# One exponential per attention chunk in a fused attention and gated FFN kernel: differences and sums on VectorE, weight words converted in place

## The chip, the cores and the metric

The kernel runs on one core of a Trainium2 chip. The metric is device time in microseconds (us) of one launch. The kernel before takes 1119.18 us, the median of 3 runs (1118.94 to 1120.06).

The engines go by the profile's names: PE is TensorE (PEld its weight loads), DVE is VectorE, ACT is ScalarE, POOL is GpSimd, SP is SyncE, whose queue issues the DMAs.

## The reference

```python
# q, k, v: (8, 8, 576, 64) float32, S = 576, pool = 8, Sp = 72
k_p = k.reshape(B, H, Sp, pool, D).mean(axis=3)
v_p = v.reshape(B, H, Sp, pool, D).mean(axis=3)
scores = scale * np.matmul(q, k_p.transpose(0, 1, 3, 2))
scores = scores - np.max(scores, axis=-1, keepdims=True)
attn = np.exp(scores)
attn = attn / (np.sum(attn, axis=-1, keepdims=True) + 1e-09)
out = np.matmul(attn, v_p).astype(np.float32)
# x = out with heads side by side: (4608, 512)
a = x @ w_a            # (512, 1536)
b = x @ w_b
return (a * b @ w_out).astype(np.float32)
```

Keys and values are averaged in groups of eight, so each of the 64 pairs of batch and head attends with 576 queries to 72 keys. The 4608 tokens of 512 numbers then go through an FFN with two input matrices, whose products are multiplied, and one output matrix. The three weight matrices arrive as float64 and are used as float32.

## The kernel before, in words

**Precision.** Every matmul runs in the float32r format, with each operand split into a high part (a cast by ScalarE) and a low part (the difference, on VectorE or GpSimd), and three products: high x high, high x low, low x high. That is why things come in pairs: qh and ql, xh and xl, hh and hl, jha and jla.

**The FFN loop.** The tokens are worked through in 9 tiles of 512 (NT), each in 12 steps f of 128 inner columns. In `ffn_in` a step makes psa (12 matmuls of 512 columns, lines 522 to 524) and psb (12 more). ScalarE copies psa to h (L527), VectorE multiplies psb into h (L500, in `gated`), ScalarE casts hh (L503), VectorE makes hl (L170, the line of every low part). `ffn_out` adds the product with the output matrix to four PSUM banks acc (12 matmuls, lines 543 to 545), one step late.

**The attention.** The queries of a batch are cut into five chunks of 128 or 64 rows (`chunks_of`); there are 40 chunks i. Chunks 0 to 3 belong to tile 0 and are done ahead of the FFN loop (`early`), chunks 4 to 8 to tile 1, and chunks 9 to 39 to the tiles from 2 on: 25 of these have 128 rows and six have 64. The generator `chunk(i)` does one chunk: it loads the queries (tile qraw), makes qh (L356) and ql, and then the scores. Two head groups g (two heads each) share one PSUM tile psc: three matmuls of 144 columns for each g (L379), whose loaded operand is the queries and whose moving operand is kdiag, the pooled keys with a high part (w = 0) and a low part (w = 1). VectorE takes the maximum of each head (L388) and scales it by -1/8 (L389); ScalarE then makes one exponential for each head with that bias, which also adds up the head's sum z (L392). After both pairs VectorE adds 1e-9 to z and inverts it (L399, L400), GpSimd (VectorE for two early chunks) multiplies s by it (L402), ScalarE casts the high parts pr and rem (L411, L413), and GpSimd makes their low parts. Three rounds of transposes follow (ptr, L447, copied to p by ScalarE, L448), then the product with the values vdiag and vrem (po, lines 480 to 483), and xh and xl (L491, L170).

The banks for psc, ptr and po come from the tag "att" with two buffers (the early chunks take psc from "acc", with four). A tile is free again when its last reader is done.

**Keys and values.** `load_keys(b)` and `load_values(b)` load a batch's keys and values and pool them on VectorE (L253, L305). At the end `load_values` makes vwide (L314), vdiag (L328) and vrem on VectorE in three neighbouring steps.

**Weights.** `convert_weights` runs in tile 0 for each matrix (a, b, o): a DMA brings 512 KB of 64-bit words into `words`, one for each f; ScalarE shrinks the high words into a temporary `wmag` (L210) and the low words into `wlow` (L211); VectorE masks and shifts `wmag` into the weights' place (L212), adds the sign (L216) and adds the low word (L221). The next words of a matrix are asked for only after L216. `split_weight` makes the high and low parts of a weight; for the matrices a and b in tile 0 the low part (jla, jlb) is VectorE's, else GpSimd's (L235).

**What sets the order.** The program is written out in one fixed order for every engine. The class `Chains` holds all generators as chains: each runs until a `yield`, which gives the number of steps it sleeps, or until `yield PE`, by which it asks for a place among the matmuls. The FFN loop calls `chains.step()` once every six of its matmuls, six times an f, and each call takes up the chains that are due and one that asks for PE. So one more `yield 1` in a chunk moves all that follows it on by one step, behind what other chains and the FFN issue on the same engine.

Of the kernel before, what the change touches and what calls it, by code (L numbers as in the profile page):

```python
# [11 lines left out]
I32 = mybir.dt.int32  # L12
# [40 lines left out]
BLOCK, BLOCK_LATER = 256, 384  # L53

NTMP = 6

AHEAD = 2

# [12 lines left out]
class Chains:  # L71
# [9 lines left out]
    def mark(self, *what):  # L81
        self.done.add(what)
# [30 lines left out]
def attn_moe_kernel(ctx: ExitStack, tc: tile.TileContext, q, k, v, vr, wa, wb, wo, out):  # L113
# [80 lines left out]
    def convert_weights(name, j, first):  # L194

        def load_words(f):
            nc.sync.dma_start(area[name], w_dram[name][:, f, :].bitcast(I32))  # L200

        load_words(0)
        yield first
        for f in range(NF):
            words = area[name].rearrange("p (c w) -> p c w", w=2)
            hi, lo = words[:, :, 1], words[:, :, 0]
            w = raw[name][:, f, :]
            wi = w.bitcast(I32)
            low, mag = tmp(f"wlow_{name}{f}", I32), tmp(f"wmag_{name}{f}")
            nc.scalar.activation(mag, hi.bitcast(F32), AF.Abs, scale=SHRINK)  # L210
            nc.scalar.activation(low, lo.bitcast(U32), AF.Copy, scale=2.0**-29)  # L211
            nc.vector.tensor_scalar(  # L212
                out=wi, in0=mag.bitcast(I32), scalar1=0x0FFFFFFF, scalar2=3, op0=ALU.bitwise_and, op1=ALU.logical_shift_left
            )
            yield 1
            nc.vector.scalar_tensor_tensor(  # L216
                out=wi, in0=hi, scalar=-(1 << 31), in1=wi, op0=ALU.bitwise_and, op1=ALU.bitwise_or
            )
            if f + 1 < NF:
                load_words(f + 1)  # L220
            nc.vector.tensor_tensor(out=wi, in0=wi, in1=low, op=ALU.add)  # L221
            mark("weight", name, f)
            yield 2

            while f + 1 >= AHEAD and (len(begun) <= f + 1 - AHEAD or chains.now < begun[f + 1 - AHEAD] + 2 * j):
                yield 1
# [116 lines left out]
    def chunk(i):  # L343
# [22 lines left out]
        z = sb.tile([P, H], F32, tag="z", name=f"z_{i}")  # L366
        hk = 2 * SP

        for g0 in range(0, NK, 2):
            yield from wait(("keys", b, g0))  # L370
            yield PE
            if first:
                pt = ps.tile([P, 512], F32, tag="acc", name=f"psc_{i}_{g0}", bufs=4)
            else:
                pt = ps.tile([P, 512], F32, tag="att", name=f"psc_{i}_{g0}", bufs=2)
            for j in range(2):
                g = g0 + j
                for x, (qq, w) in enumerate(((qh, 0), (qh, 1), (ql, 0))):
                    nc.tensor.matmul(  # L379
                        pt[:n, j * hk:(j + 1) * hk],  # L380
                        qq[:, g, :n],
                        kd[:, g, w].rearrange("p e s -> p (e s)"),
                        start=(x == 0),
                        stop=(x == 2),
                    )
            hs = slice(2 * g0, 2 * g0 + 4)
            scores = pt[:n, :2 * hk].rearrange("p (h s) -> p h s", h=4)
            nc.vector.tensor_reduce(out=m[:n, hs], in_=scores, axis=AX.X, op=ALU.max)  # L388
            nc.vector.tensor_scalar_mul(m[:n, hs], m[:n, hs], -SCALE)  # L389
            for j in range(4):  # L390
                h = 2 * g0 + j
                nc.scalar.activation(  # L392
                    s[:n, h], scores[:, j], AF.Exp, bias=m[:n, h:h + 1], scale=SCALE, accum_out=z[:n, h:h + 1]
                )
        mark("scores", i)


        yield 1
        nc.vector.tensor_scalar_add(z[:n], z[:n], 1e-9)  # L399
        nc.vector.reciprocal(z[:n], z[:n])  # L400
        yield 1
# [254 lines left out]
```

## Time and profile before

| | |
|---|---|
| median of 3 runs | 1119.18 us (1118.94 to 1120.06) |
| the profiled execution | 1116.74 us, of which the span of its instructions is 1115.0 |
| mean granted clock of TensorE | 0.986 |
| instructions | 14406 |
| share of the chain that ended last | PE 78%, DVE 13%, ACT 6%, issue 2%, DMA 1% |
| DMA | 59.64 MB, mean 53 GB/s |

The profile is one execution. Its span runs from the first instruction to the end of the last. Row counts such as x432 are instructions; "idle before" is the time the engine stood still just ahead of them, with what ended it. The chain is followed back from the last instruction, at each step to what released it. Three stages are told apart: 0 to 60 us (the front: early chunks, first weight words), 60 to 209 us (tile 0) and 209 us to the end. Line numbers here and in the prediction are those of the kernel before.

### The profile page before, as it was taken

To read this page: it belongs to the slowest core of one execution; us is meant where nothing else is said; L and a number is where in the kernel's file an instruction comes from. 1 tells how busy PE (TensorE), PEld (TensorE's weight loads), DVE (VectorE), ACT (ScalarE), POOL (GpSimd) and SP (SyncE) were. 2 spreads that over 40 slices of the span, in tenths; PEclk is the share of its full clock that TensorE was granted. 3 is DMA by queue.
4 is the path that set the end of the run, shared out by engine and by line. 5 is a ranking of instruction groups with operands and counts; after the bars stand their busy time and mean duration, and the time that the engine had idled before them with its cause. 6 is when DMAs were issued, how large, how long until landed. Compare 5 with 4: busy or idle time off the path is not lost.

```text
span 1115.0 us, 14406 instructions
## 1 busy us (share of the span) xinstructions
PE 1045.9 (94%) x5088; PEld 870.9 (78%) x5088; DVE 543.8 (49%) x839; ACT 594.8 (53%) x1651; POOL 538.6 (48%) x441
## 2 busy tenths in 40 slices
PE   4387888999998999999999999999999999999998
PEld 4276666888887888888887888888887888888887
DVE  7688888632455225632456335643356333332111
ACT  5756766545555455554556455554555455453332
POOL 7102322555555555555556455545546555554442
PEclk9989889999999999999999999999999999999999
DMA  6454443210112001300030003200211020001001
GB/s 209 131 160 123 124 150 126 73 42 1 55 42 85 1 1 41 130 1 1 22 115 14 1 2 102 68 1 1 69 55 48 1 66 1 2 1 38 1 1 38
DMA packets 29879, 59.64 MB, mean 53 GB/s; under 512 B 7120, under 2 KB 7120, under 8 KB 29808
## 3 DMA queue, kind: packets, MB, share of 16 engines
q1 hardware_dynamic: 29808, 58.73, 16.5%
q8 instruction: 40, 0.66, 0.3%
q14 instruction: 31, 0.25, 0.1%
HBM read 49.28 MB, written 9.44 MB: 53 GB/s over the span
## 4 chain that ended last, share of the span: by engine, by line
PE 78%; DVE 13%; ACT 6%; issue 2%; DMA 1%; SPq 0%; DVEq 0%; ACTq 0%
PE psb L522 8%; PE psa L522 8%; PE psa L524 8%; PE psa L523 8%; PE acc L543 8%; PE acc L544 8%; PE acc L545 8%; PE psb L524 8%; PE psb L523 7%; PE psc L379 3%; ACT s L392 3%; DVE vdiag L328 2%; PE ptr L447 2%; DVE vrem L170 1%; DVE h L500 1%
## 5 line engine op out<-in xcount | busy, mean ns | idle before, releaser
L500 DVE TENSOR_TENSOR h<-psb,h 128x512 f32<-128x512 f32 x108 | 74.5, 690 | 310.7 <-PE psb L524 310.6
L170 POOL TENSOR_TENSOR jlb<-wb_raw,jhb 128x512 fp32r<-128x512 f32 x96 | 125.1, 1303 | 201.2 <-ACT jhb L233 201.2
L170 POOL TENSOR_TENSOR jlo<-wo_raw,jho 128x512 fp32r<-128x512 f32 x108 | 152.7, 1414 | 81.0 <-ACT jho L233 51.8
L522 PE MATMUL psb<-xh,jhb 128*128 128x512 f32 x432 | 177.8, 412 | 1.3 <-DVE h L500 1.3
L524 PE MATMUL psb<-xh,jlb 128*128 128x512 f32 x432 | 171.5, 397 | 1.8 <-DVE jlb L170 1.8
L522 PE MATMUL psa<-xh,jha 128*128 128x512 f32 x432 | 172.3, 399 | 0.0
L543 PE MATMUL acc<-jho,hh 128*128 128x512 f32 x432 | 171.5, 397 | 0.0
L527 ACT COPY h<-psa 128x512 f32<-128x512 f32 x108 | 63.5, 588 | 201.9 <-PE psa L524 188.4
L523 PE MATMUL psb<-xl,jhb 128*128 128x512 f32 x432 | 170.8, 395 | 0.0
L524 PE MATMUL psa<-xh,jla 128*128 128x512 f32 x432 | 170.1, 394 | 0.0
L523 PE MATMUL psa<-xl,jha 128*128 128x512 f32 x432 | 169.6, 393 | 0.0
L544 PE MATMUL acc<-jlo,hh 128*128 128x512 f32 x432 | 169.5, 392 | 0.0
L545 PE MATMUL acc<-jho,hl 128*128 128x512 f32 x432 | 169.2, 392 | 0.0
L392 ACT ACTIVATE s<-psc,m 128x72 f32<-128x72 f32 (+1 forms) x320 | 97.9, 318 | 133.1 <-DVE m L389 131.7
L170 POOL TENSOR_TENSOR jla<-wa_raw,jha 128x512 fp32r<-128x512 f32 x96 | 138.4, 1442 | 44.1 <-ACT jha L233 43.7
L402 POOL TENSOR_TENSOR s<-s,z 128x576 f32<-128x576 f32 (+1 forms) x38 | 46.1, 1213 | 223.7 <-PE psb L524 141.0
L170 DVE TENSOR_TENSOR hl<-h,hh 128x512 fp32r<-128x512 f32 x108 | 125.8, 1165 | 38.2 <-ACT hh L503 38.0
L503 ACT CAST hh<-h 128x512 fp32r<-128x512 f32 x108 | 67.1, 622 | 89.4 <-DVE h L500 89.2
L524 PEld LDWEIGHTS psb<-xh,jlb 128*128 128x128 f32 x432 | 82.4, 191 | 20.8 <-DVE jlb L170 2.7
L524 PEld LDWEIGHTS psa<-xh,jla 128*128 128x128 f32 x432 | 81.9, 190 | 17.5
L545 PEld LDWEIGHTS acc<-jho,hl 128*128 128x128 f32 x432 | 81.8, 189 | 17.4
L543 PEld LDWEIGHTS acc<-jho,hh 128*128 128x128 f32 x432 | 81.9, 190 | 16.2
(84 smaller groups left out, 1806.3 us busy)
## 6 DMA issues: line engine op xcount, KB each, us to landing
out<-y SPq DMA_DIRECT2D x36, 256.0 KB, 2.1
kraw<-in_k SPq DMA_DIRECT2D x28, 288.0 KB, 3.4
vraw<-in_v SPq DMA_DIRECT2D x28, 256.0 KB, 3.3
qraw<-in_q SPq DMA_DIRECT2D x28, 256.0 KB, 3.7
words<-in_wa SPq DMA_DIRECT2D x12, 512.0 KB, 3.7
words<-in_wb SPq DMA_DIRECT2D x12, 512.0 KB, 3.6
words<-in_wo SPq DMA_DIRECT2D x12, 512.0 KB, 3.6
vraw<-in_vr SPq DMA_DIRECT2D x14, 192.0 KB, 2.7
```

Of the source, the lines that this page charges most:

```text
L170: eng.tensor_tensor(out=lo, in0=src, in1=hi.bitcast(F32), op=ALU.subtract)
L392: nc.scalar.activation(s[:n, h], scores[:, j], AF.Exp, bias=m[:n, h:h + 1], scale=SCALE, accum_out=z[:n, h:h + 1])
L402: (nc.vector if first and i % 2 else nc.gpsimd).tensor_tensor(out=s[:n], in0=s[:n], in1=z[:n].unsqueeze(2).broadcast_to([n, H, SP]), op=AL ...
L500: nc.vector.tensor_tensor(out=h, in0=pt, in1=h, op=ALU.mult)
L503: nc.scalar.copy(hh, h)
L522: nc.tensor.matmul(pt, wh[:, c], xh[:, kk], start=(kk == 0), stop=False)
L523: nc.tensor.matmul(pt, wh[:, c], xl[:, kk], start=False, stop=False)
L524: nc.tensor.matmul(pt, wl[:, c], xh[:, kk], start=False, stop=(kk == NK - 1))
L527: nc.scalar.copy(h, pt)
L543: nc.tensor.matmul(acc[c], hh[:, cs], wh, start=(f == 0), stop=False)
L544: nc.tensor.matmul(acc[c], hh[:, cs], wl, start=False, stop=False)
L545: nc.tensor.matmul(acc[c], hl[:, cs], wh, start=False, stop=(f == NF - 1))
```

## The change

There are three parts.

1. In `convert_weights` ScalarE writes the shrunk high words into the weights' own place, and VectorE masks and shifts them there. The temporary `wmag` is gone.
2. The softmax: the new `less_max` takes the maximum of each head and subtracts it, both on VectorE, and writes the differences to s. Then one exponential over all eight heads (576 numbers a row) is made by ScalarE in place, and VectorE adds up z.
3. Chunks from 9 on (SUMMED) make their scores otherwise: one matmul of 288 columns takes qh with the high and the low keys side by side, one of 144 takes ql with the high keys on top of the first half, and VectorE adds the two halves of the bank into s (a reduction over pairs). Each g has a bank of its own, two g are taken in one place among the matmuls. `less_max` then runs once on s.

The words given with the change also name lo parts of two matrices on VectorE in the first tile; that line (L235) is the same in both kernels.

```diff
+SUMMED = 9
...
-            low, mag = tmp(f"wlow_{name}{f}", I32), tmp(f"wmag_{name}{f}")
-            nc.scalar.activation(mag, hi.bitcast(F32), AF.Abs, scale=SHRINK)
+            low = tmp(f"wlow_{name}{f}", I32)
+            nc.scalar.activation(w, hi.bitcast(F32), AF.Abs, scale=SHRINK)
...
-                out=wi, in0=mag.bitcast(I32), scalar1=0x0FFFFFFF, scalar2=3, op0=ALU.bitwise_and, op1=ALU.logical_shift_left
+                out=wi, in0=wi, scalar1=0x0FFFFFFF, scalar2=3, op0=ALU.bitwise_and, op1=ALU.logical_shift_left
...
-            nc.vector.tensor_reduce(out=m[:n, hs], in_=scores, axis=AX.X, op=ALU.max)
-            nc.vector.tensor_scalar_mul(m[:n, hs], m[:n, hs], -SCALE)
-            for j in range(4):
-                h = 2 * g0 + j
-                nc.scalar.activation(
-                    s[:n, h], scores[:, j], AF.Exp, bias=m[:n, h:h + 1], scale=SCALE, accum_out=z[:n, h:h + 1]
+        def less_max(hs, src):
+            nh = hs.stop - hs.start
+            nc.vector.tensor_reduce(out=m[:n, hs], in_=src, axis=AX.X, op=ALU.max)
+            nc.vector.tensor_tensor(
+                out=s[:n, hs], in0=src, in1=m[:n, hs].unsqueeze(2).broadcast_to([n, nh, SP]), op=ALU.subtract
+            )
+
+        if i < SUMMED:
...
+                less_max(slice(2 * g0, 2 * g0 + 4), pt[:n, :2 * hk].rearrange("p (h s) -> p h s", h=4))
+        else:
+            for g in range(NK):
+                yield from wait(("keys", b, g - g % 2))
+                if g % 2 == 0:
+                    yield PE
+                pt = ps.tile([P, 512], F32, tag="att", name=f"psc_{i}_{g}", bufs=2)
+                nc.tensor.matmul(
+                    pt[:n, :2 * hk], qh[:, g, :n], kd[:, g].rearrange("p w e s -> p (w e s)"), start=True, stop=False
                 )
+                nc.tensor.matmul(
+                    pt[:n, :hk], ql[:, g, :n], kd[:, g, 0].rearrange("p e s -> p (e s)"), start=False, stop=True
+                )
+                nc.vector.tensor_reduce(
+                    out=s[:n, 2 * g:2 * g + 2, :].rearrange("p h s -> p (h s)"),
+                    in_=pt[:n, :2 * hk].rearrange("p (w c) -> p c w", w=2),
+                    axis=AX.X,
+                    op=ALU.add,
+                )
+                if g % 2 and g < NK - 1:
+                    yield 1
+            yield 1
+            less_max(slice(0, H), s[:n])
         mark("scores", i)
...
         yield 1
+        nc.scalar.activation(s[:n], s[:n], AF.Exp, scale=SCALE)
+        yield 1
+        nc.vector.tensor_reduce(out=z[:n], in_=s[:n], axis=AX.X, op=ALU.add)
         nc.vector.tensor_scalar_add(z[:n], z[:n], 1e-9)
         nc.vector.reciprocal(z[:n], z[:n])
```

How the change moves instructions is seen in the order in which each engine gets them. A row is the line, the operation, output and inputs (with running numbers) and the shape of the output. On TensorE, at the first place of scores of a chunk in the third tile, before (psc are the scores of two head groups, psa and psb the FFN's):

```order
L524 MATMUL psa_5_3437<-xh_2027,jla_3385 128x512
L379 MATMUL psc_0_3451<-kdiag_74,qh_3418 128x144 x2
L379 MATMUL psc_0_3451<-kdiag_74,ql_3419 128x144
L379 MATMUL psc_0_3451<-kdiag_74,qh_3418 128x144 x2
L379 MATMUL psc_0_3451<-kdiag_74,ql_3419 128x144
L522 MATMUL psa_5_3437<-xh_2027,jha_3384 128x512
```

The same place after, with the second one, six FFN matmuls on:

```order
L403 MATMUL psc_0_3319<-kdiag_74,qh_3286 128x288
L406 MATMUL psc_0_3319<-kdiag_74,ql_3287 128x144
L403 MATMUL psc_1_3323<-kdiag_74,qh_3286 128x288
L406 MATMUL psc_1_3323<-kdiag_74,ql_3287 128x144
L549 MATMUL psa_5_3305<-xh_1952,jha_3252 128x512
L550 MATMUL psa_5_3305<-xl_1953,jha_3252 128x512
L551 MATMUL psa_5_3305<-xh_1952,jla_3253 128x512
L549 MATMUL psa_5_3305<-xh_1952,jha_3252 128x512
L550 MATMUL psa_5_3305<-xl_1953,jha_3252 128x512
L551 MATMUL psa_5_3305<-xh_1952,jla_3253 128x512
L403 MATMUL psc_2_3337<-kdiag_74,qh_3286 128x288
L406 MATMUL psc_2_3337<-kdiag_74,ql_3287 128x144
```

Six matmuls in one bank have become four in two banks, and psc_2 takes the bank of psc_0 again.

On VectorE, at the end of the values load in the third tile beside a chunk of 64 rows, before (hl and h are the FFN's, z the sums of the chunk, vwide, vdiag and vrem the values load's):

```order
L170 TENSOR_TENSOR hl_3011<-h_2971,hh_3010 128x512
L399 TENSOR_SCALAR z_3021<-z_3021 64x8
L400 RECIPROCAL z_3021<-z_3021 64x8
L314 SCALAR_TENSOR_TENSOR vwide_3085<-vp_2842,mask 96x256 x2
L328 SCALAR_TENSOR_TENSOR vdiag_76<-vp_2842,vdiag_76 64x4x64 x2
L170 TENSOR_TENSOR vrem_2841<-vwide_3085,vrem_2841 32x512
L500 TENSOR_TENSOR h_3107<-psb_1_3109,h_3107 128x512
```

And after (L172 is the line of the low parts, L527 that of h):

```order
L172 TENSOR_TENSOR hl_2873<-h_2844,hh_2872 128x512
L316 SCALAR_TENSOR_TENSOR vwide_2934<-vp_2714,mask 96x256 x2
L330 SCALAR_TENSOR_TENSOR vdiag_76<-vp_2714,vdiag_76 64x4x64 x2
L409 TENSOR_REDUCE s_2881<-psc_2_2960 64x144
L409 TENSOR_REDUCE s_2881<-psc_3_2964 64x144
L373 TENSOR_REDUCE m_2882<-s_2881 64x8
L374 TENSOR_TENSOR s_2881<-s_2881,m_2882 64x576
L172 TENSOR_TENSOR vrem_2713<-vwide_2934,vrem_2713 32x512
L527 TENSOR_TENSOR h_2974<-psb_1_2976,h_2974 128x512
L425 TENSOR_REDUCE z_2883<-s_2881 64x8
L426 TENSOR_SCALAR z_2883<-z_2883 64x8
L427 RECIPROCAL z_2883<-z_2883 64x8
```

The z steps have moved from ahead of the values load to behind the next h, and four operations on the scores stand between vdiag and h.

On ScalarE, where it first comes to weight words, before (p are the transposed weights of attention, pr and rem their high parts):

```order
L448 COPY p_0_283<-ptr_0_335 128x4x128
L448 COPY p_0_311<-ptr_1_343 128x4x128
L448 COPY p_0_325<-ptr_2_349 96x2x128
L411 CAST pr_353<-s_250 128x512
L413 CAST rem_354<-s_250 128x2x32 x2
L210 ACTIVATE wmag_a_359<-words 128x512
```

And after:

```order
L475 COPY p_0_263<-ptr_0_311 128x4x128
L475 COPY p_0_289<-ptr_1_319 128x4x128
L212 ACTIVATE wa_raw<-words 128x512
L213 ACTIVATE wlow_a_325<-words 128x512
L475 COPY p_0_300<-ptr_2_330 96x2x128
L438 CAST pr_334<-s_235 128x512
```

The first words stand ahead of the third copy of transposes and of the last early chunk's casts.

More of the change, by code (lines that the diff above doesn't have):

```diff
@@ L367, in chunk @@
         hk = 2 * SP
[L369 to L389, printed above, removed]
-            for j in range(4):
-                h = 2 * g0 + j
-                nc.scalar.activation(
-                    s[:n, h], scores[:, j], AF.Exp, bias=m[:n, h:h + 1], scale=SCALE, accum_out=z[:n, h:h + 1]
-                )
@@ new lines, in less_max @@
+        def less_max(hs, src):
[5 more added lines that the diff above has]
+        if i < SUMMED:
+            for g0 in range(0, NK, 2):
+                yield from wait(("keys", b, g0))
+                yield PE
+                if first:
+                    pt = ps.tile([P, 512], F32, tag="acc", name=f"psc_{i}_{g0}", bufs=4)
+                else:
+                    pt = ps.tile([P, 512], F32, tag="att", name=f"psc_{i}_{g0}", bufs=2)
+                for j in range(2):
+                    g = g0 + j
+                    for x, (qq, w) in enumerate(((qh, 0), (qh, 1), (ql, 0))):
+                        nc.tensor.matmul(
+                            pt[:n, j * hk:(j + 1) * hk],
+                            qq[:, g, :n],
+                            kd[:, g, w].rearrange("p e s -> p (e s)"),
+                            start=(x == 0),
+                            stop=(x == 2),
+                        )
+                less_max(slice(2 * g0, 2 * g0 + 4), pt[:n, :2 * hk].rearrange("p (h s) -> p h s", h=4))
+        else:
+            for g in range(NK):
+                yield from wait(("keys", b, g - g % 2))
+                if g % 2 == 0:
+                    yield PE
+                pt = ps.tile([P, 512], F32, tag="att", name=f"psc_{i}_{g}", bufs=2)
+                nc.tensor.matmul(
+                    pt[:n, :2 * hk], qh[:, g, :n], kd[:, g].rearrange("p w e s -> p (w e s)"), start=True, stop=False
+                )
+                nc.tensor.matmul(
+                    pt[:n, :hk], ql[:, g, :n], kd[:, g, 0].rearrange("p e s -> p (e s)"), start=False, stop=True
[5 more added lines that the diff above has]
+                    op=ALU.add,
+                )
+                if g % 2 and g < NK - 1:
+                    yield 1
+            yield 1
+            less_max(slice(0, H), s[:n])
```

## The prediction

> **What bounds the kernel now.** I read the page first, then busy time by stage, then the chain and the waits of each stage.
>
> ```profile
> span 1115.0 us, 14406 instructions
> PE 1045.9 (94%) x5088; PEld 870.9 (78%) x5088; DVE 543.8 (49%) x839; ACT 594.8 (53%) x1651; POOL 538.6 (48%) x441
> ```
>
> The first row is the span, the second each engine's busy time. TensorE (PE) is busy 94% of the span, VectorE (DVE) and ScalarE (ACT) about half. But 69 us of TensorE's time are idle, and an average doesn't say where. The stages do (start:end, length, busy time of PE, PEld, DVE, ACT, POOL, then granted clock, DMA share, GB/s):
>
> ```profile
> 0.00:60.00 60.00, 25.43 (x121) 23.30 (x122) 42.11 (x79) 35.82 (x121) 24.03 (x33) 1.00 0.55 178
> 60.00:209.00 149.00, 127.42 (x591) 101.60 (x591) 123.68 (x207) 100.79 (x268) 36.96 (x29) 0.92 0.40 125
> 209.00:1115.00 906.00, 893.04 (x4380) 745.99 (x4378) 378.02 (x554) 458.22 (x1263) 477.64 (x380) 1.00 0.10 34
> ```
>
> Three kernels in one. In the last 906 us TensorE idles 13 us: only fewer matmuls, or the few stalls, can gain there. In the front (60 us, before the first FFN matmul) and in the first tile (149 us) TensorE idles 35 and 22 us; there VectorE is the fullest engine, or nearly so (42 of 60 us, 124 of 149), and what it or ScalarE loses can reach the end.
>
> **The change part by part.** *Fewer matmuls in the scores of chunks 9 to 39.* A slot of two head groups had six matmuls of 144 columns; now it has two of 288 and two of 144. The trace's timeline (start, duration, instruction) gives the pace of each size as the step from start to start, the last row of each fence being the FFN matmul that follows. Six of 144 columns, 128 query rows:
>
> ```profile
> 573.87 0.34 PE L379 MATMUL psc<-kdiag,qh 128*128 128x144 f32 x2
> ...
> 574.49 0.43 PE L522 MATMUL psb<-xh,jhb 128*128 128x512 f32 x1
> ```
>
> The same six for a chunk of 64 rows:
>
> ```profile
> 602.67 0.30 PE L379 MATMUL psc<-kdiag,qh 128*64 128x144 f32 x2
> ...
> 603.07 0.44 PE L522 MATMUL psa<-xh,jha 128*128 128x512 f32 x1
> ```
>
> Eight of 256 columns:
>
> ```profile
> 482.81 0.28 PE L480 MATMUL po<-p,vdiag 128*128 128x256 f32 x1
> ...
> 483.76 0.40 PE L522 MATMUL psb<-xh,jhb 128*128 128x512 f32 x1
> ```
>
> And four of 384:
>
> ```profile
> 304.31 0.34 PE L480 MATMUL po<-p,vdiag 128*128 128x384 f32 x1
> ...
> 305.02 0.40 PE L522 MATMUL psb<-xh,jhb 128*128 128x512 f32 x1
> ```
>
> Six matmuls of 144 columns take 574.49 - 573.87 = 0.62 us with 128 query rows, 0.103 each; with 64 rows 0.40, 0.067 each. Same moved columns, other time: at this size the number of query rows, which are the loaded columns, sets the pace. Eight of 256 columns take 0.95, 0.119 each; four of 384 take 0.71, 0.178 each. Between them, 288 columns come to 0.134. So a slot costs 2 x (0.134 + 0.103) = 0.474 in place of 0.62, and 0.146 is saved: two slots a chunk, 25 chunks of 128 rows, 7.3 us. If 288 ran like 384, a slot saves 0.06: 3 us; if like 256, 0.176: 8.8 us. The six chunks of 64 rows gain nothing (two of 0.134 for four of 0.067). The saving is on the path, since TensorE ends last there.
>
> The Trainium skill, "TensorE: Matmul & The Clock Gate", gives N/2.4 + 2.5 ns as the warm gap of a matmul of N columns ("Back-to-back issue gap") and P/1.2 ns for loading P columns ("LDWEIGHTS (loading the stationary operand)"). By these the 144-column matmul is held by its load at 107 ns, the 288-column one takes 122.5, and the saving is 8.05 us, an estimate; the rows above agree with the load rule (0.103 and 0.067 for 128 and 64 rows), and my sum stays with them.
>
> *ScalarE loses the exponentials by head.* These are the forms that go, and those from which the new ones are priced (busy time, mean ns | idle before):
>
> ```profile
> L392 ACT ACTIVATE s<-psc,m 128x72 f32<-128x72 f32 x256 | 78.5, 321 | 110.6 <-DVE m L389 109.4 <-PE psa L524 1.2
> L392 ACT ACTIVATION_READ_ACCUMULATOR s<-psc,m 128x1 f32 x256 | 52.5, 205 | 0.0
> L411 ACT CAST pr<-s 128x512 fp32r<-128x512 f32 x32 | 19.7, 617 | 0.1
> L388 DVE TENSOR_REDUCE m<-psc 128x4 f32<-128x288 f32 x64 | 29.2, 456 | 61.8 <-PE psc L379 61.5
> L389 DVE TENSOR_SCALAR m<-m 128x4 f32<-128x4 f32 x64 | 13.4, 209 | 2.2
> L253 DVE TENSOR_REDUCE kp<-kraw 128x72 f32<-128x576 f32 x28 | 20.1, 740 | 1.8 <-DMA kraw<-in_k 1.8
> L402 DVE TENSOR_TENSOR s<-s,z 128x576 f32<-128x576 f32 x2 | 1.5, 754 | 0.1
> ```
>
> Eight exponentials and eight accumulator reads a chunk, 8 x 0.321 = 2.6 us if the reads overlap (at most 8 x 0.526 = 4.2), become one of 576 elements. 512 take 0.617, so 0.69 in proportion. After 209 us ScalarE works half the time, and these 1.9 us a chunk are worth nothing by themselves. Before it they lie on the chain:
>
> ```profile
> by line: ACT s L392 12.1%; DMA wb_raw<-in_k 8.7%; DMA words<-in_wb 6.5%; DMA words<-in_wo 5.9%; DMA words<-in_wa 5.9%; DVE vdiag L328 4.7%; DVE kp L253 4.7%; DVE m L389 4.5%; issue 4.5%; ACT p L448 4.0%; DVE vp L305 3.0%; ACT kdiag L264 3.0
> 37.03 0.68 ACT L210 ACTIVATE wmag_a<-words 128x512 f32<-128x512 f32 x1
> 39.82 3.53 DMA words<-in_wa
> 50.93 3.56 DMA words<-in_wo
> ```
>
> *Front.* The first row is the front's chain: 12.1% of 60 us, 7.3 us, is exponentials. The first weight words are taken by ScalarE at 37.03, behind the softmax of the early chunks; then word loads of 3.5 us follow each other, each issued once the words before are converted, nearly up to the first FFN matmul. With two chunks' exponentials (5.1 us) cut to 1.4, ScalarE gets to the words some 3.7 us earlier. VectorE, which must mask them, gains less: it adds 1.3 us a chunk (below). I take -3, the smaller part of the 7.3: bounds -6 and +0.8 (VectorE's own queue sets everything).
>
> *First tile.* VectorE gains per chunk two subtractions from PSUM (priced like the 0.456 maximum) and one sum over 576 (0.74), and loses two scalings (0.2): 0.91 + 0.74 - 0.4 = +1.25, over five chunks +6.3 us if VectorE is the bound. Against that stand its own waits on ScalarE:
>
> ```profile
> DVE z L399 <- ACT s L392: 7.8, 6, 1.5
> DVE wo_raw L212 <- ACT wmag_o L210: 4.9, 2, 2.5
> DVE wb_raw L212 <- ACT wmag_b L210: 3.8, 2, 1.9
> ```
>
> The first (in total, times, longest) is VectorE waiting for exponentials; the others for weight words behind them in ScalarE's queue, 8.7 together. The first goes, and six of the 8.7, as the exponentials shrink from 13 us (5 x 2.6) to 3.5. New is the wait of the sum for the one exponential, with the step order putting other work before it: 4 us. Sum 6.3 - 7.8 - 6 + 4 = -3.5. Bounds: -10 (the new wait is hidden, all waits go) and +6.3.
>
> *Words in the weights' place, lo parts.* The mask reads and writes the same place: same count and sizes, and no row shows ScalarE waiting for a temporary; 0. The two matrices' lo parts of the first tile are on VectorE already before, so that part of the description changes nothing: 0. SP's order of loads and stores is untouched.
>
> *VectorE after 209 us.* Each chunk gains four sums of pairs (like the 0.456 maximum: 288 elements read), one maximum over 576 (0.74), a subtraction of 576 from SBUF (0.75 to 1.9, below) and one sum (0.74), and loses two maxima and two scalings: about +3 us. The cover:
>
> ```profile
> DVE h L500 <- PE psb L524: 308.8, 88, 7.5
> PE ptr L447 <- ACT p L448: 8.6, 6, 3.5
> ```
>
> VectorE idles 309 us there waiting for TensorE's psb; 31 chunks of 3 us fit three times over. So 0, except where VectorE's run is already late.
>
> The subtraction's row is the other operation with two SBUF inputs:
>
> ```profile
> L170 DVE TENSOR_TENSOR hl<-h,hh x108: 675/1027/2701, 73.5 to 1107.2; 128x512 fp32r<-128x512 f32 x108
> ```
>
> 0.675 at the least, 2.7 at the most (minimum/median/maximum): it is slowed beside POOL's work, so 576 elements cost 0.75 to about 1.9. The Trainium skill, "SBUF — State Buffer", "Who interferes with whom", says why this part speaks against the change: a VectorE instruction with two SBUF inputs contends with a GpSimd instruction that reads SBUF, under an exclusive lock, while a reduction never does; the spread of the row agrees. By the rule 31 subtractions take turns with POOL, up to some 2 us each; behind the cover above that makes no difference, so my sum leaves it at 0.
>
> *The stalls at values loads.* The six waits in the last row, 8.6 us together, are TensorE's transposes waiting for the copy of the last ones. One of them:
>
> ```profile
> 335.97 6.81 DVE L328 SCALAR_TENSOR_TENSOR vdiag<-vp,vdiag 64x256 fp32r<-64x256 f32 x2
> 343.41 0.69 DVE L500 TENSOR_TENSOR h<-psb,h 128x512 f32<-128x512 f32 x1
> 345.17 0.36 PE L447 MATMUL ptr<-ident,rem 64*96 64x64 f32 x2 [3.52 <-ACT p L448]
> ```
>
> A values load holds VectorE 6.8 us, the FFN's h is late, ScalarE's cast of h blocks the copy of the transposes, and TensorE stands. At three such places (chunks of 64 rows) two sums, a maximum and a subtraction now stand between vdiag and h, about 2.4 us less the z pair (0.4) that moves behind: 2.0; POOL's multiplication by 1/z, which ran beside vdiag, comes later and frees part: +1.2 each, +3.6. At the three others the transposes stand two steps later, behind the late run: their waits go: the five others average 1.0, and I take 0.7 for these, -2.1. Net +1.5; bounds -10 (all stalls and the slow clock behind them go) and +9 (3 us more at each of three).
>
> **Sum.** -7.3 - 3 - 3.5 + 1.5 = -12.3 us. The profiled execution took 1116.74, span 1115.0 and 1.7 around it; the median of the runs, 1119.18, is 2.4 above it. Profiled 1104.5; median 1119.2 - 12.3 = 1107.0 (to the nearest half).
>
> **The rivals.** *TensorE waits for the sums of pairs (slower).* Two banks hold the four score groups of a chunk, so the third group's matmuls wait until VectorE has summed the first, the fourth's for the second's. The fourth may start 2.06 us after the first: two pairs (0.474), six FFN matmuls (1.36), the third's pair (0.237). VectorE may be in hl when the scores come:
>
> ```profile
> 946.97 1.78 DVE L170 TENSOR_TENSOR hl<-h,hh 128x512 fp32r<-128x512 f32 x1
> 948.03 0.34 PE L379 MATMUL psc<-kdiag,qh 128*128 128x144 f32 x2
> ```
>
> Here hl ends 0.72 after the scores begin. With sums of d each and 0.06 of signalling the stall is 0.72 + 2d + 0.06 - 2.06. At d = 0.46 that is -0.36: none. It starts at d = 0.64, and eats the whole 12.3 us (0.49 in each of 25 chunks) at 0.89. A sum of 144 strided pairs isn't in the trace; the reduction rows (288 to 4 in 0.456, 576 to 72 in 0.740) show no charge for an output. If each of 144 outputs cost as much as four elements more (about 1 ns an element between those rows), d = 1.0, 0.72 a chunk, 18 us: 1125. Against it: no such charge in either row. Chance 0.10.
>
> *The front and the first tile give nothing back.* VectorE is the fullest engine there and gets 1.25 us more a chunk: +0.8 + 6.3 - 7.3 + 1.5 = +1.3: 1120.5, no change that could be told. For it: 124 of 149 us busy. Against it: 16 of its 25 idle us there are waits for ScalarE. Chance 0.08.
>
> *The stalls all go.* The later transposes then miss the late runs altogether: -10 in place of +1.5, 1095.5. Against it: three runs of VectorE get longer. Chance 0.07.
>
> **How the numbers follow.** The forecast itself has 0.75, its unknowns carrying it from about 1099 to 1115. A measurement can tell some 0.2% (2.2 us) from no change. Faster: forecast and third rival, 0.82; same: the second, 0.08; slower: the first, 0.10. The range takes in the third rival's better part and the bad ends of the first tile and stalls: 1094 to 1117, leaving out the first two, 0.18.
>
> **What would show it.** Right: TensorE's busy time after the first tile down by 7 us, with 31 x 12 score matmuls become 31 x 8; psc_2 without a wait; the first FFN matmul 3 us ahead of its 60; the waits of z on exponentials shrunk in the first tile. Wrong: sums of pairs near 1 us and TensorE waiting at the third or fourth scores; a first tile still 149 us long; waits of ptr longer than 3.5 us.

## The result and the profile after

The changed kernel takes 1088.24 us, the median of 4 runs (1087.65 to 1089.28), against 1119.06 (1118.61 to 1120.06): a ratio of 0.9724, 95% interval 0.9708 to 0.9741. It is 30.8 us faster; 12 were forecast, and the time lies below the range. One of the runs below, the first of the kernel with two later steps, took 1332.85 us at a granted clock of 0.735; it is left out of that kernel's time, and its trace isn't used. The profiled execution of the changed kernel took 1088.67, with this span and these busy times:

```profile
span 1086.9 us, 13596 instructions
PE 1029.8 (95%) x4964; PEld 856.0 (79%) x4964; DVE 580.4 (53%) x941; ACT 523.3 (48%) x1051; POOL 531.7 (49%) x441
```

TensorE has 16 us less to do and VectorE 37 more, as its extra operations ask. The stages, cut where the first FFN matmul and the second tile begin (start:end, length, busy PE, PEld, DVE, ACT, POOL, granted clock, DMA share, GB/s):

```profile
0.00:58.60 58.60, 25.57 (x120) 23.18 (x121) 48.35 (x83) 28.56 (x61) 23.00 (x33) 0.87 0.56 182
58.60:203.00 144.40, 124.19 (x589) 99.59 (x588) 131.19 (x211) 89.01 (x177) 38.85 (x29) 0.94 0.41 129
203.00:1086.90 883.90, 880.04 (x4259) 733.20 (x4257) 400.81 (x648) 405.68 (x814) 469.80 (x379) 1.00 0.11 34
```

Against before (60, 149 and 906 us) the front gave 1.4, the first tile 4.6 and the rest 22.1 us. These add up to 28.1 and not to 30.8, since the profiled execution of before (1116.74) was faster than the median. Of the 22.1, 13.0 are TensorE's busy time (893.04 to 880.04) and 9.1 its idle time (12.96 to 3.86). The idle time that went is the six waits of the transposes ptr for the copies of p, 8.6 us before; the trace of after has no wait of TensorE left behind 203 us. Where a few matmuls in a row ran at 0.43 us a step behind such a wait (0.23 is usual), their time counted as busy, so a part of the 13.0 belongs to the waits too.

Why did they go? These are the rows of the groups concerned (busy, mean ns | idle before), first those of before that are to be compared:

```profile
L328 DVE SCALAR_TENSOR_TENSOR vdiag<-vp,vdiag 64x256 fp32r<-64x256 f32 x16 | 27.2, 1700 | 0.2
L170 DVE TENSOR_TENSOR vrem<-vwide,vrem 32x512 fp32r<-32x512 f32 x8 | 11.0, 1380 | 0.0
```

And after:

```profile
L409 DVE TENSOR_REDUCE s<-psc 128x144 f32<-128x288 f32 x100 | 41.1, 451 | 54.0 <-PE psc L406 53.6
L374 DVE TENSOR_TENSOR s<-s,m 128x576 f32<-128x576 f32 x25 | 28.3, 1133 | 0.9
L330 DVE SCALAR_TENSOR_TENSOR vdiag<-vp,vdiag 64x256 fp32r<-64x256 f32 x16 | 10.5, 658 | 0.2
L172 DVE TENSOR_TENSOR vrem<-vwide,vrem 32x512 fp32r<-32x512 f32 x8 | 5.5, 684 | 0.2
```

The sum of pairs costs what the forecast said, 0.451 us, and the subtraction of 576 lies in its bounds. But vdiag, whose instructions are the same in both kernels, fell from a mean of 1.700 us to 0.658, and vrem from 1.380 to 0.684. The prediction set no rows of GpSimd beside them. In the trace of before, from 335.97 to 342.78 us, while VectorE is in the two vdiag operations, GpSimd's timeline (start, duration, instruction, idle before) is:

```profile
335.57 1.49 POOL L402 TENSOR_TENSOR s<-s,z 64x576 f32<-64x576 f32 x1 [4.40 <-DVE z L400]
337.02 1.29 POOL L170 TENSOR_TENSOR jla<-wa_raw,jha 128x512 fp32r<-128x512 f32 x1
338.40 1.36 POOL L170 TENSOR_TENSOR pr<-s,pr 64x512 fp32r<-64x512 f32 x1
339.71 0.33 POOL L170 TENSOR_TENSOR rem<-s,rem 64x64 fp32r<-64x64 f32 x1
339.99 1.28 POOL L170 TENSOR_TENSOR jlb<-wb_raw,jhb 128x512 fp32r<-128x512 f32 x1
341.24 1.25 POOL L170 TENSOR_TENSOR jlo<-wo_raw,jho 128x512 fp32r<-128x512 f32 x1
```

The inversion of z, the instruction just ahead of vwide and vdiag on VectorE, starts the multiplication on GpSimd, and five more operations follow it almost without a gap. VectorE's two take 6.81 us beside them: 2.63 and 4.15, and each ends 0.29 us behind the end of a GpSimd operation (jla at 338.31, jlo at 342.49). At the same load of after, VectorE and GpSimd:

```profile
324.58 1.91 DVE L330 SCALAR_TENSOR_TENSOR vdiag<-vp,vdiag 64x256 fp32r<-64x256 f32 x2
324.92 1.29 POOL L172 TENSOR_TENSOR jla<-wa_raw,jha 128x512 fp32r<-128x512 f32 x1 [3.06 <-PE psc L406]
326.52 0.81 DVE L409 TENSOR_REDUCE s<-psc 64x144 f32<-64x288 f32 x2
327.37 0.75 DVE L373 TENSOR_REDUCE m<-s 64x8 f32<-64x576 f32 x1
328.15 0.75 DVE L374 TENSOR_TENSOR s<-s,m 64x576 f32<-64x576 f32 x1
328.93 0.68 DVE L172 TENSOR_TENSOR vrem<-vwide,vrem 32x512 fp32r<-32x512 f32 x1
329.65 0.69 DVE L527 TENSOR_TENSOR h<-psb,h 128x512 f32<-128x512 f32 x1
```

One operation of GpSimd lies beside vdiag now. From the start of vdiag to the h behind it VectorE needs 5.1 us, with four operations more, where before it needed 7.4. All the traces used here, sixteen, say the same of vdiag's length: the 106 vdiag operations with no GpSimd operation beside them took 0.40 to 0.43 us, the 28 beside three or four took 1.68 to 4.15. So the theory to test is: **the steps put in ahead of z moved GpSimd's run off vdiag**. Its rivals: ScalarE without the eight exponentials has the copies of p done in time; or the transposes, two steps later, miss VectorE's late run however long it is.

And the slots of the scores, after, at 128 rows:

```profile
475.54 0.29 PE L403 MATMUL psc<-kdiag,qh 128*128 128x288 f32 x1
475.67 0.23 PE L406 MATMUL psc<-kdiag,ql 128*128 128x144 f32 x1
475.74 0.34 PE L403 MATMUL psc<-kdiag,qh 128*128 128x288 f32 x1
475.92 0.23 PE L406 MATMUL psc<-kdiag,ql 128*128 128x144 f32 x1
475.98 0.44 PE L549 MATMUL psb<-xh,jhb 128*128 128x512 f32 x1
```

0.44 us in place of 0.62 from the first of them to the FFN matmul behind; the forecast had 0.474.

### The profile page after: what moved, and what is told of

It is laid out like the page before. It is cut to its first block, busy times and chain, and to the rows that moved or that the text cites. A ratio compares the mean times of both kernels' runs of the same rounds, so it can differ in the third digit from the quotient of the medians.

```text
span 1086.9 us, 13596 instructions
## 1 busy us (share of the span) xinstructions
PE 1029.8 (95%) x4964; PEld 856.0 (79%) x4964; DVE 580.4 (53%) x941; ACT 523.3 (48%) x1051; POOL 531.7 (49%) x441
## 4 chain that ended last, share of the span: by engine, by line
PE 84%; DVE 9%; ACT 3%; DMA 2%; issue 1%; POOL 0%; SPq 0%; DVEq 0%; ACTq 0%; POOLq 0%
PE acc L570 9%; PE psa L549 9%; PE acc L572 8%; PE psa L551 8%; PE acc L571 8%; PE psb L549 8%; PE psa L550 8%; PE psb L551 8%; PE psb L550 8%; PE ptr L474 3%; PE psc L403 2%; DVE wb_raw L218 1%; PE po L509 1%; PE po L510 1%; PE psc L406 1%
## 5 line engine op out<-in xcount | busy, mean ns | idle before, releaser
L527 DVE TENSOR_TENSOR h<-psb,h 128x512 f32<-128x512 f32 x108 | 74.5, 690 | 343.7 <-PE psb L551 326.6
L172 POOL TENSOR_TENSOR jlb<-wb_raw,jhb 128x512 fp32r<-128x512 f32 x96 | 125.6, 1309 | 218.2 <-ACT jhb L235 218.2
L172 POOL TENSOR_TENSOR jla<-wa_raw,jha 128x512 fp32r<-128x512 f32 x96 | 126.5, 1317 | 140.9 <-ACT jha L235 117.9
L172 POOL TENSOR_TENSOR jlo<-wo_raw,jho 128x512 fp32r<-128x512 f32 x108 | 154.2, 1428 | 82.4 <-ACT jho L235 74.8
L570 PE MATMUL acc<-jho,hh 128*128 128x512 f32 x432 | 174.3, 404 | 0.0
L549 PE MATMUL psb<-xh,jhb 128*128 128x512 f32 x432 | 171.6, 397 | 1.9 <-DVE h L527 1.9
L172 DVE TENSOR_TENSOR hl<-h,hh 128x512 fp32r<-128x512 f32 x108 | 91.6, 848 | 20.8 <-ACT hh L530 20.6
L549 PEld LDWEIGHTS psb<-xh,jhb 128*128 128x128 f32 x432 | 81.5, 189 | 17.5 <-issue 2.3
L429 POOL TENSOR_TENSOR s<-s,z 128x576 f32<-128x576 f32 (+1 forms) x38 | 52.3, 1376 | 86.3 <-DVE z L427 48.8
L549 PEld LDWEIGHTS psa<-xh,jha 128*128 128x128 f32 x432 | 81.7, 189 | 15.3
```

What stands on the lines that cost most here:

```text
L172: eng.tensor_tensor(out=lo, in0=src, in1=hi.bitcast(F32), op=ALU.subtract)
L429: (nc.vector if first and i % 2 else nc.gpsimd).tensor_tensor(out=s[:n], in0=s[:n], in1=z[:n].unsqueeze(2).broadcast_to([n, H, SP]), op=AL ...
L527: nc.vector.tensor_tensor(out=h, in0=pt, in1=h, op=ALU.mult)
L549: nc.tensor.matmul(pt, wh[:, c], xh[:, kk], start=(kk == 0), stop=False)
L570: nc.tensor.matmul(acc[c], hh[:, cs], wh, start=(f == 0), stop=False)
```

## The experiments

Each was timed beside the kernel before on the same chip; the times of before in these series have medians of 1117.9 to 1118.8.

**Two steps later, and nothing else.**

```diff
+        if i >= 9:
+            yield 1
         mark("scores", i)
         yield 1
+        if i >= 9:
+            yield 1
         nc.vector.tensor_scalar_add(z[:n], z[:n], 1e-9)
```

> Edit: the kernel before with two more steps in the chunks from 9 on (one ahead of the mark of the scores, one ahead of the sum's 1e-9), so that the multiplication by 1/z on GpSimd and all behind it stand two steps later, as in the changed kernel; matmuls and exponentials stay. Theory (contention: the values load's vdiag on VectorE took up to 6.8 us because GpSimd's run of multiplication and low parts stood beside it, and the later steps move that run behind it): vdiag falls from a mean of 1.7 us to under 0.8 after 209 us, the waits of ptr on the copies of p (8.6 us) go, and the time falls by 10 to 13 us to 1106 to 1109. Rival (it was ScalarE's shorter queue without the eight exponentials that let the copies of p come in time): vdiag and the waits stay, 1117 to 1121.

1108.64 us, ratio 0.9903 (0.9888 to 0.9918), 10.0 us down. The kernel was run again for its trace.

> The kernel before with two more steps in the chunks from 9 on, once more, for its profile: about 1108.8; vdiag between 0.41 and 1.4 us, waits of ptr on the copies of p gone or under 3 us.

1107.80. Waits of TensorE behind 203 us (total, times, longest), and the vdiag group:

```profile
PE ptr L451 <- ACT s L392: 2.6, 3, 1.0
PE ptr L451 <- ACT p L452: 1.0, 1, 1.0
L328 DVE SCALAR_TENSOR_TENSOR vdiag<-vp,vdiag 64x256 fp32r<-64x256 f32 x16 | 12.8, 801 | 0.3
```

The waits for p fell from 8.6 to 1.0 with all exponentials in place: a shorter queue of ScalarE isn't needed for that. The mean of vdiag is 0.80, from 1.70 (the 16 include the four of the first two loads, ahead of 209 us). New is a small wait of ptr behind the exponentials (2.6), which now stand near the transposes.

**The same work, the values loads earlier.**

```diff
-KEYS_AHEAD, VALUES_AFTER = 18, 16
+KEYS_AHEAD, VALUES_AFTER = 18, 10
```

> Edit: one number of the kernel before: the values loads of batches 2 to 7 start 10 steps behind the keys in place of 16, so that vdiag stands ahead of the inversion of z on VectorE and GpSimd's run starts behind it. All work is the same. Theory of contention: vdiag under 0.8 us, stalls of ptr gone, time 10 to 13 us down, 1106 to 1109, as in the kernel with two more steps. Rival of ScalarE's queue: no change, 1117 to 1121. Rival of the order (transposes that stand later miss VectorE's late run, whatever makes it long): also down, but with vdiag as long as before.

1106.11, ratio 0.9887 (0.9874 to 0.9901), 12.5 us down, and the vdiag group:

```profile
L328 DVE SCALAR_TENSOR_TENSOR vdiag<-vp,vdiag 64x256 fp32r<-64x256 f32 x16 | 8.7, 544 | 0.3
```

After 209 us every vdiag takes 0.41 to 0.42 us, and no wait of ptr is left. One number of the program, no instruction more or less, is worth more than my whole forecast. The chunks' own steps stand as in the kernel before, so "later transposes" isn't needed to explain it either. Of what it gains beyond the 8.6 us of waits some 2 us are slow steps behind them: behind 209 us 22 matmuls of 512 columns had a step near 0.43 us in the trace of before, 13 have it here. This run doesn't separate one thing: the load moved away from the transposes as well as from GpSimd's run. The next run leaves the load in its place.

**vdiag on GpSimd.**

```diff
+            if b > 1:
+                nc.gpsimd.tensor_scalar_mul(vp[r, :NK], vp[r, :NK], 1.0 / POOL)
+                low_part(nc.gpsimd, vd[r, :, 1, r], vp[r, :NK], vd[r, :, 0, r])
+            else:
...
```

> Edit: the kernel before with the two vdiag differences of batches 2 to 7 on GpSimd (a scaling and a subtraction each) in place of VectorE; nothing else moves. It takes 0.83 us of undisturbed work off VectorE in each of six loads, and adds some 5 us to GpSimd's queue there. Theory of contention: VectorE is no longer held for up to 6.8 us, h comes in time, and the stalls of ptr at the chunks of 64 rows shrink from 1.7 to 3.7 us to under 1; time down by 5 to 11 us, 1108 to 1114. Against it: the low parts of weights behind it in GpSimd's queue may come late and take back some. Rival of the order: vdiag's place stays, the transposes wait as before, 1117 to 1120.

1125.01, ratio 1.0058 (1.0044 to 1.0071): slower, against both. Its first wait of TensorE behind 209 us:

```profile
PE ptr L451 <- POOL pr L170: 10.4, 6, 2.4
```

The waits for p are gone, though the load and the transposes keep their place: taking vdiag off VectorE did free it. But the low part pr of the chunk, behind vdiag in GpSimd's queue, is now late at the same six places. The theory's part is seen, the time is not evidence for it.

**The contention brought back in the changed kernel.**

```diff
-KEYS_AHEAD, VALUES_AFTER = 18, 16
+KEYS_AHEAD, VALUES_AFTER = 18, 19
```

> Edit: one number of the changed kernel: the values loads of batches 2 to 7 start 19 steps behind the keys in place of 16, which puts the inversion of z straight ahead of vdiag again at the chunks of 64 rows, so that GpSimd's multiplication and low parts run beside vdiag. All work is the same. Theory of contention: vdiag again 1.4 to 4 us at those three places, waits of ptr for copies of p come back, time up by 5 to 12 us, 1093 to 1100. Rival of ScalarE's queue (no eight exponentials, no stall): 1087 to 1090.

1102.46, ratio to before 0.9854 (0.9841 to 0.9868): 14.2 us given back by three steps, more than I expected, and in another way. Both vdiag operations take 1.27 to 1.28 us at the three places (one of the two did before), and no ptr waited for p. What happened, VectorE, GpSimd and TensorE in the changed kernel with the later loads:

```profile
334.86 1.29 POOL L172 TENSOR_TENSOR pr<-s,pr 64x512 fp32r<-64x512 f32 x1 [0.73 <-ACT pr L438]
334.91 3.30 DVE L172 TENSOR_TENSOR vrem<-vwide,vrem 32x512 fp32r<-32x512 f32 x1
336.11 0.31 POOL L172 TENSOR_TENSOR rem<-s,rem 64x64 fp32r<-64x64 f32 x1
336.39 1.26 POOL L172 TENSOR_TENSOR jla<-wa_raw,jha 128x512 fp32r<-128x512 f32 x1
338.24 0.69 DVE L172 TENSOR_TENSOR hl<-h,hh 128x512 fp32r<-128x512 f32 x1
338.84 1.76 DVE L409 TENSOR_REDUCE s<-psc 64x144 f32<-64x288 f32 x4
339.34 0.35 PE L403 MATMUL psc<-kdiag,qh 128*64 128x288 f32 x1 [2.50 <-DVE s L409]
```

It was vrem that met GpSimd's run: 3.30 us for an operation of 0.68. Behind it stand hl and the four sums of pairs, and TensorE's third scores waited 2.5 us for a bank. This is the wait of the first rival, brought on by the contention. Over the kernel behind 203 us:

```profile
PE psc L403 <- DVE s L409: 7.5, 3, 2.5
PE psc L406 <- DVE ql L172: 2.0, 3, 0.7
PE ptr L474 <- DVE s L409: 0.7, 1, 0.7
```

These are 10.2 of the 14.2 us, all of them waits for a late VectorE; the two profiled executions (1100.46 and 1088.67) are 11.8 apart.

**Sums of pairs twice.**

```diff
+                for _ in range(2):
                     nc.vector.tensor_reduce(
                         out=s[:n, 2 * g:2 * g + 2, :].rearrange("p h s -> p (h s)"),
...
```

> Edit: the changed kernel with each sum of pairs done twice, the second time over the same place. This is the price of my first rival: TensorE waits for the sums. A sum measured 0.45 us, so now 0.9 a bank. By the prediction's formula the stall is 0.72 + 2 x 0.9 + 0.06 - 2.06 = 0.52 us where hl stands as late as it can, in at most 25 chunks: up to 13 us, 1088 to 1101. If hl is mostly early, as the trace of before had it in most chunks: 1088 to 1092. Over 1101: the sums are nearer to the limit than the formula says.

1106.05, 17.8 us above the changed kernel. The wait appears at once:

```profile
PE psc L403 <- DVE s L410: 8.8, 33, 0.6
```

The rival was real, and dearer than the 13 us that its formula gave here for a sum of 0.9. By the trace's timeline the second place of scores of most chunks of 128 rows takes 0.83 us in place of 0.44: 0.39 a chunk, where the formula had 0.52, about 10 us in all. The chunks of 64 rows, for which the formula has no term, add about 4, and the first tile about 2. The rival did not happen because the sum measured 0.45.

**The new matmuls with the old softmax and the old steps.**

```diff
...
+            nc.vector.tensor_reduce(out=m[:n], in_=s[:n], axis=AX.X, op=ALU.max)
+            nc.vector.tensor_scalar_mul(m[:n], m[:n], -SCALE)
+            for h in range(H):
+                nc.scalar.activation(s[:n, h], s[:n, h], AF.Exp, bias=m[:n, h:h + 1], scale=SCALE, accum_out=z[:n, h:h + 1])
...
```

> Edit: the kernel before with the new matmuls and sums of pairs in the chunks from 9 on, but the exponentials by head, the scaled maximum and the steps as before. The sum of the pairs is in SBUF, the maximum over eight heads and the exponentials read it there. Theory (the slots are a separate gain): TensorE's slots cost 0.45 us in place of 0.64, about 10 us in 62 slots, while vdiag stays slow and the stalls stay: 1108 to 1110. My prediction's term of 7.3 would give 1112. Rival (the sums of pairs on VectorE make other things late): over 1114.

1149.71, ratio 1.0276 (1.0261 to 1.0291): 31 us slower. With the maximum over all heads, all eight exponentials stand behind the last scores, where half of them could start after the first pair. GpSimd's work and the transposes keep their old places and aren't ready for them. Waits of TensorE behind 209 us:

```profile
PE ptr L472 <- ACT p L473: 16.5, 6, 4.0
PE ptr L472 <- POOL pr L170: 13.1, 25, 0.6
```

So this run can't show the gain of the slots alone. These two rows, 29.6 us, are nearly the whole loss; that the shorter softmax or the later steps would take them away was not tried apart.

**The changed kernel with the old matmuls.**

```diff
-SUMMED = 9
+SUMMED = 40
...
+        if i >= 9:
+            yield 1
         mark("scores", i)
```

> Edit: the changed kernel with the old twelve matmuls of 144 columns in all chunks (the differences then come from PSUM by pairs, without sums of pairs), and one step put in so that the rest of chunks 9 to 39 keeps its place. Theory (the slots give 10 us of their own, measured between the two profiles as 37.1 to 26.9 us in the slots of the scores): 1088.2 + 10 = 1098, 1096 to 1100. By my prediction's term of 7.3: 1095.5. Rival (the slots bring more, since VectorE's later place or the second bank matters too): over 1102; or less, under 1094.

1097.79, ratio 0.9816 (0.9802 to 0.9829). The slots are worth 1097.8 - 1088.2 = 9.6 us.

**Chunks 0 to 8 alone, chunks 0 to 3 alone, words alone.** The new code in chunks below 9 or below 4 (and the words in place), the old in the others; or only the words:

```diff
-        if i < SUMMED:
+        if i < 9:
...
```

> Edit: the kernel before with the change in chunks 0 to 8 and in the weight words alone; chunks 9 to 39 are as before. Theory (from the two profiles: the first FFN matmul comes 1.3 us earlier, the second tile starts 6.2 us earlier): 1118.6 - 6.2 = 1112.4, 1110 to 1115. My prediction had -3 - 3.5 = -6.5 for the same parts. Rival (what the first tile gains is in part lost by the kernel as a whole, or needs the later chunks too): over 1116.

1112.42, ratio 0.9944 (0.9931 to 0.9958): 5.5 us down.

> Edit: the kernel before with the words in place and the new softmax in the four early chunks alone. The run with chunks 0 to 8 took 1112.4, 5.5 under before. Theory A (the gain of that run is ScalarE's queue in the first tile, chunks 4 to 8, whose exponentials VectorE's z and the words waited for): about 1117, most of the 5.5 missing. Theory B (the front: the early chunks' exponentials are gone ahead of the first words): 1112 to 1114.

1118.75, ratio 0.9998 (0.9990 to 1.0007): nothing.

> Edit: the kernel before with the weight words scaled into the weights' place, and nothing else. Prediction: 0, 1117.5 to 1120. Rival: without the temporary the six buffers of that pool are free earlier, and loads and conversions in the first tile move up: 1113 to 1116. Other rival: ScalarE now writes a place that VectorE's last work on it or the early queries hold, and waits: over 1121.

1118.76, ratio 1.0005 (0.9995 to 1.0014): nothing, as forecast. The early chunks gave nothing by themselves. In the run with chunks 0 to 3 ScalarE takes the first words at 33.69, where it was 37.03 before, and the front is 1.1 us shorter, but the first tile is 2 us longer:

```profile
33.69 0.68 ACT L210 ACTIVATE wa_raw<-words 128x512 f32<-128x512 f32 x1
...
0.00:58.90 58.90, 25.66 (x121) 23.26 (x122) 48.05 (x83) 28.56 (x61) 23.05 (x33) 0.87 0.57 184
58.90:210.10 151.20, 127.21 (x591) 101.09 (x591) 123.59 (x207) 100.66 (x268) 37.58 (x29) 0.93 0.39 122
```

The 5.5 need the chunks of the first tile. VectorE's waits in the first tile of the run with chunks 0 to 8:

```profile
DVE wb_raw L212 <- ACT wb_raw L210: 3.1, 2, 2.2
DVE z L430 <- ACT s L419: 1.5, 1, 1.5
DVE wo_raw L212 <- ACT wo_raw L210: 1.4, 2, 0.7
```

The wait of z for exponentials fell from 7.8 to 1.5, those for weight words from 8.7 to 4.5.

**The new matmuls in the first tile too.**

```diff
-SUMMED = 9
+SUMMED = 4
```

> Edit: one number of the changed kernel, SUMMED = 4 in place of 9: the chunks 4 to 8, done in the first tile, take the new matmuls too. TensorE saves 0.37 us in each of four chunks of 128 rows, 1.5 us; VectorE, the fullest engine there, gains four sums (1.8 us) and 0.6 in each of five chunks, up to 12 us where nothing covers it. If VectorE sets the first tile's end: 1090 to 1100. If TensorE does: 1086 to 1088.

1099.04, ratio 0.9813 (0.9793 to 0.9834), 10.8 us above the changed kernel. The first tile is 156 us long in place of 144:

```profile
58.00:214.00 156.00, 129.72 (x567) 102.04 (x567) 133.58 (x222) 90.45 (x178) 38.65 (x29) 0.90 0.38 119
```

The five chunks (three of 128 rows, two of 64) cost 12 us there, but not as VectorE's busy time: that rose by 2.4 us, from 131.19 to 133.58, while VectorE's idle time rose from 13.2 to 22.4. TensorE now waits for sums of pairs in this stage, which it did not in the changed kernel:

```profile
PE ptr L474 <- DVE s L409: 8.9, 2, 4.7
PE psc L403 <- DVE s L409: 4.9, 2, 3.2
```

So the sums stand on the path between TensorE and VectorE there, as in the first rival; how much of the 12 us is theirs was not tried apart.

**Earlier values loads in the changed kernel.**

```diff
-KEYS_AHEAD, VALUES_AFTER = 18, 16
+KEYS_AHEAD, VALUES_AFTER = 18, 10
```

> Edit: one number of the changed kernel: the values loads start 10 steps behind the keys in place of 16, the number that took 12.5 us off the kernel before. In the changed kernel vdiag is short already (0.41 to 1.48 us) and no wait of ptr is left after the first tile. Theory of contention: nothing is left to gain, 1087 to 1089.5. If 10 steps gain something else than the contention: under 1086. If vrem or vdiag meets GpSimd's run at the new place: over 1091.

1089.90, ratio to before 0.9743 (0.9730 to 0.9757): 1.7 us above the changed kernel, nothing gained; vrem meets GpSimd there (a mean of 1.18 us, from 0.68). The number that gave 12.5 in the kernel before has nothing left to remove. No version tried beats the changed kernel.

**What the later steps leave.** Two kernels with the change in chunks 0 to 8, old matmuls and exponentials by head behind it, and the contention removed in the one way or the other:

> Edit: the change in chunks 0 to 8 and in the words, and the two later steps in chunks 9 to 39, which keep their old matmuls and exponentials by head. It differs from the kernel with old matmuls (1097.8) only in how chunks 9 to 39 make their softmax: maximum, scaling and eight exponentials, or maximum, subtraction, one exponential and one sum. If the two parts add up: 1118.6 - 5.5 - 9.9 = 1103.2. Theory A (the eight exponentials still cost something on ScalarE): 1101 to 1105. Theory B (the later steps are all of it, and the 9.9 was small because of the run): 1097 to 1099.

1101.31, ratio 0.9851 (0.9838 to 0.9864).

> Edit: the change in chunks 0 to 8 and in the words, old chunks from 9 on with their old steps, and the values loads 10 steps behind the keys in place of 16, by which vdiag was 0.41 us everywhere. If the parts add up: 1118.6 - 5.5 - 12.5 = 1100.6. Theory A (what is left to 1097.8 is ScalarE's): 1099.5 to 1102. Theory B (contention is all of it): 1097 to 1099.

1099.71, ratio 0.9831 (0.9818 to 0.9844). The kernel with old matmuls and the new softmax in all chunks had 1097.79. So 1.9 to 3.5 us are left for the exponentials of chunks 9 to 39 themselves. In the kernel with the later steps TensorE's transposes wait 2.6 us for exponentials and 1.0 us for a copy of p behind 203 us; the kernel with the new softmax in all chunks has no wait there. So the 3.5 are mostly transposes that, two steps later, stand close behind the exponentials.

## Why the prediction was wrong

Going from one kernel to the next by single edits, the gain is made up like this:

| edit | us |
|---|---|
| words, and the softmax of chunks 0 to 8 (1117.9 to 1112.4) | 5.5 |
| two steps later in chunks 9 to 39 (to 1101.3) | 11.1 |
| one exponential in these chunks (to 1097.8) | 3.5 |
| new matmuls in these chunks (to 1088.2) | 9.6 |

The sum is 29.7; the 30.8 of the result go from a median of before that lay 1.1 higher. The runs come from several series. Against the kernel before of its own series each, the four terms are 5.5, 11.6, 3.0 and 10.7, so a term is known to about 1 us.

- **The slots: the mechanism right, the term too small.** -7.3 was forecast, 9.6 measured. The step of 288 columns is shorter than I put it: a slot takes 0.44 and not 0.474. A saving of 0.18 in 50 slots makes 9.0. The estimate of 8.05 from the Trainium skill ("TensorE: Matmul & The Clock Gate", "Back-to-back issue gap" and "LDWEIGHTS (loading the stationary operand)") was nearer, but it set the page's figures for the new slot against the measured 0.62 of the old one; with the page's figures for both (0.64 and 0.46) the estimate is 9.1. The prediction's row of 64 query rows (0.067 a matmul) does not agree with the load rule, which gives 0.053; the page's gap for 144 columns, 0.0625, is nearer. Chunks of 64 rows gained nothing in their slots, as forecast.
- **The front: wrong.** -3 was forecast, the early chunks alone gave 0.0. ScalarE did come to the words 3.3 us earlier, nearly the 3.7 of the text; but VectorE is busy 48 of 59 us there now (42 of 60 before), the first FFN matmul gained 1.1, and the first tile took that back. The text had this as the other end of the range.
- **The first tile: right.** -3.5 forecast; chunks 0 to 8 gave 5.5 with the front's share at nothing, by the waits of z and of the words that were named.
- **Words, lo parts, VectorE's 3 us a chunk behind 209 us: right**, at 0.
- **ScalarE's exponentials behind 209 us: too small.** They were put at nothing, since ScalarE works half the time there; 1.9 to 3.5 us were measured.
- **The stalls at the values loads: here the prediction failed.** "Net +1.5" took the 6.8 us of vdiag as a length that nearly stays. At three loads it added 2.0 us of VectorE's work and let GpSimd's later multiplication free 0.8; at the three others it kept VectorE's late run as it was and let the transposes miss it. But the length was the doing of GpSimd's whole run, and the change moves all of it: at the load shown vdiag fell from 6.81 to 1.91 us. In the kernel before, two steps alone take 10.0 us off, and an earlier load 12.5, with vdiag back at 0.4 us in the second case. Of the 18.5 us that the forecast missed, 12.6 lie here (11.1 gained, 1.5 lost in the forecast). I had the Trainium skill's rule on the exclusive lock ("SBUF — State Buffer", "Who interferes with whom") in the text, and used it against the new subtraction only; vdiag has two SBUF inputs as well, and the trace of before agrees with the rule there: 6.81 us for two operations that take 0.41 each where GpSimd is idle. It goes beyond the rule in that one operation of VectorE stood behind several of GpSimd's in a row. GpSimd's rows beside vdiag's, in the trace of before, were what could have shown it. The third rival (all stalls go, 1095.5, chance 0.07) named the effect for another reason, and with 2.3 us more for the slots and 3.5 for one exponential it would have been about 1090.
- **The first rival** didn't come, and its mechanism is real: the sums done twice cost 17.8 us. That this is near the 18 that the prediction gave for a sum of 1.0 is in part luck: the chunks of 128 rows gave less than the formula says for 0.9, the chunks of 64 rows, which it left out, the rest.

What stays open: what the exponentials of chunks 9 to 39 would cost without the later steps; the kernel with earlier loads puts 1.9 us on them (1.4 against the kernel before of each series), and a difference of that size is at the limit of what these runs tell. Also open is why the new matmuls lengthen the first tile by 12 us, and, in the kernel with later loads, what the 1.6 us of the profiles' 11.8 are that lie outside the waits that the trace names.

## What to carry to other kernels

A duration in a profile is a length under the neighbours that it had: before pricing work ahead of or behind a long operation, see whether the same form is short elsewhere (0.41 and 4.15 us here), and what runs beside it. A change of a step can then be worth more than the operations that it was made for, and one can look for it alone: here a single number of the schedule gives 12.5 of 31 us without a new instruction. And a gain on one engine needs its partner: new matmuls with the old softmax and steps were 31 us slower, with the rest of the change 9.6 faster.

## What the hardware showed that I had not expected

Two of VectorE's operations with two SBUF inputs did not merely share time with GpSimd but waited through several of its operations in a row: vdiag 6.81 us beside a run of six, vrem 3.30 us beside three, against 0.82 (two of 0.41) and 0.68 alone. VectorE's reductions were not slowed in the changed kernel: the 124 sums of pairs, from PSUM, took 0.436 to 0.458 us, and the 31 maxima over 576 numbers in SBUF 0.741 to 0.754, with GpSimd beside them (27 of the sums, 22 of the maxima) or not. The subtraction of 576 numbers, with two inputs in SBUF, took 0.749 to 0.759 alone and up to 1.256 with GpSimd beside it.
